# Score broadcasts on GpSimd's queue, row copies for one batch only, later scatters and earlier transposes in an attention and mixture-of-depths kernel

## The chip, the cores and the metric

The kernel runs on one core of one Trainium2 chip. The metric is the device time of one execution in microseconds. Three timed runs of the kernel before gave 152.77, 153.0 and 153.94 us, median 153.0. The profiled execution has a span of 148.8 us; all positions in time below are microseconds from the start of that span.

TensorE (PE) multiplies matrices, VectorE (DVE) and ScalarE (ACT) do elementwise work, GpSimd (POOL) does casts, small copies and the issue of its own transfers, and SyncE (SP) only issues transfers.

## What is computed

There are four batches of 768 rows. Attention with 8 heads of size 64 looks at a window of 128 rows and at the first 4 rows ("sinks"). Its output `x` is stored, and then, for each batch, the 128 rows with the highest gate score go through a small two-layer network and are added to.

```
scores = q @ k.T / sqrt(64)              # kept where key < 4, or 0 <= query - key < 128
a      = softmax(scores);  x = a @ v     # x: [4, 768, 512], heads side by side
s      = x @ w_gate                      # [4, 768]
out    = x
for b in range(4):
    top = the 128 rows with the largest s[b]
    xe  = x[b, top]
    ye  = relu(xe @ w1) @ w2             # 512 -> 1024 -> 512
    out[b, top] = xe + sigmoid(s[b, top])[:, None] * ye
```

## The kernel before

The work is a list of 30 units. Units 0 to 11 are batch 0 (two halves of the heads, six blocks of 128 rows each); units 12 to 17 are batch 1, 18 to 23 batch 2, and 24 to 29 batch 3, one block of 128 rows with all heads each. Everything else is hung onto these units in four places: `before` (first), `middle` (after the score matmuls), `at` (after the unit's values and its norm) and `late` (last). Each engine executes its instructions in the order in which the program emits them.

```python
for i, (b, j, g) in enumerate(steps):
    for f in early.get(i, []): f()          # before(i, ...)
    if i: store(i - 1)                      # rows of unit i-1 to out (and a copy)
    step_scores(i + 2)                      # PE: q.k for the unit after next; ACT: exp into pt
    for f in mid.get(i, []): f()            # middle(i, ...)
    values(b, j, heads, X, g or 0)          # PE: sinks (vsk, psk), then pt @ v, into two banks X
    ...
    norm(x, heads, X)                       # DVE: reciprocal and multiply, X -> x
    for f in todo.get(i, []): f()           # at(i, ...)
    ...    gate_score(b, j, x)              # DVE: one column of scol (when g != 0)
    for f in todo_late.get(i, []): f()      # late(i, ...)
```

The q and k of a batch arrive as float32 (`raw`), are cast by GpSimd to bfloat16 (`kq`, three pairs of buffers), transposed by PE into the banks Y, and copied to SBUF (`KT`, `QT`) by DVE and ACT. A batch's first scores are emitted two units ahead of its first unit.

```python
def transposes(b, hp, bank):     # PE: 6 + 6 transposes; then the copies KT (DVE or ACT) and QT (ACT)
for b, i0 in ((1, 6), (2, 12), (3, 18)):
    for hp in range(HP):
        before(i0 + hp - 2, lambda b=b, hp=hp: cast_pair(b, hp))        # POOL
        at(i0 + hp, lambda b=b, hp=hp: transposes(b, hp, Y))
        at(i0 + hp, lambda b=b, hp=hp: sink_keys(b, hp))                # POOL
    at(i0 + 4, lambda b=b: sink_scores(b, range(HP), 0, Y))
```

To rank a score within its batch, every partition needs all 768 scores. For batches 0 and 1 the scores go out to DRAM and come back broadcast to 128 partitions:

```python
def bounce_out(b): sp.dma_start(out=srow[b, :]..., in_=st[b].scol[:, :])
def bounce_in(b):  sp.dma_start(out=sbc[:, :], in_=srow[b, :].partition_broadcast(128))
def rank_c(b, c):  dve.tensor_scalar(..., in0=sbc[:, :], scalar1=st[b].scol[:, c:c + 1], ..., op0=ALU.is_gt, ...)

for b, i, js in ((0, 12, (15, 15, 16, 17, 17, 18)), (1, 18, (20, 21, 22, 23, 24, 25))):
    middle(i, lambda b=b: bounce_out(b))
    middle(i + 1, lambda b=b: bounce_in(b))
    for c, i_c in enumerate(js):
        late(i_c, lambda b=b, c=c: rank_c(b, c))
```

For batches 2 and 3 PE spreads each column (`spread`, into bank 2) and DVE compares it (`compare`). After the ranks come `choose` (PE and DVE: the row numbers of the chosen rows; GpSimd: `gather`), `ffn_cast`, `ffn_in`, `ffn_1`, `ffn_2` and `ffn_out`. The rows of batches 1 to 3 are stored twice, to `out` and to `xrow[b]`, and gathered from the copy:

```python
def store(i):
    sp.dma_start(out=out[b, j * 128:(j + 1) * 128, :], in_=xt[(b, j)])
    if b: sp.dma_start(out=xrow[b][j * 128:(j + 1) * 128, :], in_=xt[(b, j)])
def ffn_out(b, bank):
    dve.scalar_tensor_tensor(out=y[:, :], in0=ps[:, bank, :], scalar=gt[b][:, 0:1], in1=xe[b % 3][:, :], ...)
    pool.indirect_dma_start(out=flat[0:(b + 1) * S, :], out_offset=... idx[b] ..., in_=y[:, :], ...)   # scatter
```

[...]

Of the kernel before, what the change touches and what calls it, by code (L numbers as in the profile page):

```python
# [8 lines left out]
FP32 = mybir.dt.float32  # L9
BF16 = mybir.dt.bfloat16  # L10
I32 = mybir.dt.int32
U32 = mybir.dt.uint32
# [3 lines left out]
B = 4  # L16
H = 8
S = 768
D = 64
HP = H // 2  # L20
NB = S // 128
DM = H * D
# [11 lines left out]
def kernel(  # L34
# [14 lines left out]
    pe, dve, act, pool, sp = nc.tensor, nc.vector, nc.scalar, nc.gpsimd, nc.sync  # L49
# [4 lines left out]
    jp = ctx.enter_context(tc.tile_pool(name="jp", bufs=2))  # L54
# [6 lines left out]
    X, Y = 4, 6  # L61
# [10 lines left out]
    x0 = one([128, NB, DM], FP32, "x0")  # L72
    scolb = [one([128, NB], FP32, f"scol{i}") for i in range(B)]
    xb = x0[:, 0:NB // 2, :].bitcast(BF16).rearrange("p a (t n) -> p (a t) n", t=2)
    E2 = x0[:, NB - 1, :].bitcast(BF16)[:, 0:NB * 128].rearrange("p (c n) -> p c n", n=128)
    sbc = one([128, S], FP32, "sbc")
# [8 lines left out]
    tok = [one([128, NB, 4], BF16, f"tok{i}") for i in range(B)]  # L85
    gt = [one([128, 1], FP32, f"gt{i}") for i in range(B)]
    idx = [one([128, 1], U32, f"idx{i}") for i in range(B)]
# [18 lines left out]
    tk_i = one([128, B + 1, NB], I32, "tk_i")  # L106
    flat = out.rearrange("b s d -> (b s) d")
    srow = tc.dram_tile([B, S], FP32, name="srow")
    xrow = [None] + [tc.dram_tile([S, DM], FP32, name=f"xrow{i}") for i in range(1, B)]
    idl = [None] + [x0[:, NB - 2, 8 * i:8 * i + 1].bitcast(U32) for i in range(1, B)]  # L110

    class State:
        def __init__(self, b):
# [52 lines left out]
    def transposes(b, hp, bank):  # L166
        s = st[b]
        n = slot[(b, hp)]
        for t, (src, dst) in enumerate(((kq[2 * n], s.KT), (kq[2 * n + 1], s.QT))):
            trp = ps[:, bank + t, :].bitcast(BF16).rearrange("p (c n) -> p c n", c=8)  # L170
            for c in range(NB):
                pe.transpose(out=trp[:, c, :], in_=src[:, c, :, :].rearrange("p h d -> p (h d)"),  # L172
                             identity=ident_b[:, :])
            o = dst[:, hp, :].rearrange("d (p c) -> d p c", c=NB)
            i = trp[:, 0:NB, :].rearrange("d c p -> d p c")
            if t == 0 and (b == 0 or hp % 2 == 0):
                dve.tensor_copy(out=o, in_=i)  # L177
            else:
                act.copy(out=o, in_=i)  # L179
# [123 lines left out]
                                 op0=ALU.mult, op1=ALU.add, accum_out=st[b].scol[:, j:j + 1])  # L303

    def bounce_out(b):
        sp.dma_start(out=srow[b, :].rearrange("(p c) -> p c", c=NB), in_=st[b].scol[:, :])

    def bounce_in(b):
        sp.dma_start(out=sbc[:, :], in_=srow[b, :].partition_broadcast(128))

    def rank_c(b, c):
        dve.tensor_scalar(out=junk[:, :].bitcast(BF16)[:, 0:S], in0=sbc[:, :], scalar1=st[b].scol[:, c:c + 1],  # L312
# [35 lines left out]
    def chosen(b, bank, e=E):  # L348
        t = tok[b]
        for c in range(NB):  # L350
            pe.matmul(out=ps[:, bank, 0:4], lhsT=e[:, c, :], rhs=t[:, c, :],
                      start=(c == 0), stop=(c == NB - 1))
        ch = jp.tile([128, 4], FP32, name="ch", tag="ch")
        dve.tensor_copy(out=ch[:, :], in_=ps[:, bank, 0:4])
        dve.tensor_scalar(out=(idl[b] if b else idx[0])[:, :], in0=ch[:, 0:1], scalar1=128.0, scalar2=ch[:, 1:2],
                          op0=ALU.mult, op1=ALU.add)
        if b:
            chl = x0[:, NB - 2, 32:33]
            dve.tensor_scalar_add(out=chl[:, :], in0=ch[:, 1:2], scalar1=float(b * S))
            dve.tensor_scalar(out=idx[b][:, :], in0=ch[:, 0:1], scalar1=128.0, scalar2=chl[:, 0:1],  # L360
                              op0=ALU.mult, op1=ALU.add)
        return ch
# [6 lines left out]
    def gate_end(b):  # L369
        g = gt[b]  # L370
        dve.tensor_scalar_add(out=g[:, :], in0=g[:, :], scalar1=1.0)
        dve.reciprocal(out=g[:, :], in_=g[:, :])

    def gather(b):
        src, ix = (xrow[b], idl[b]) if b else (flat, idx[0])
        pool.indirect_dma_start(out=xe[b % 3][:, :], out_offset=None, in_=src[0:S, :],
                                in_offset=bass.IndirectOffsetOnAxis(ap=ix[:, 0:1], axis=0),
                                bounds_check=S - 1, oob_is_err=False)

    def ffn_cast(b):  # L380
        pool.tensor_copy(out=xeb[:, :], in_=xe[b % 3][:, :])
# [16 lines left out]
    def ffn_2(b, half, bank):  # L398
        for f in range(4):
            fc = 4 * half + f  # L400
            pe.matmul(out=ps[:, bank, :], lhsT=hT[:, fc, :], rhs=w2_sb[:, fc, :],
                      start=(fc == 0), stop=(fc == 7))

    def ffn_out(b, bank):
        y = jp.tile([128, DM], FP32, name="y", tag="y")
        dve.scalar_tensor_tensor(out=y[:, :], in0=ps[:, bank, :], scalar=gt[b][:, 0:1], in1=xe[b % 3][:, :],  # L406
                                 op0=ALU.mult, op1=ALU.add)
        pool.indirect_dma_start(out=flat[0:(b + 1) * S, :],
                                out_offset=bass.IndirectOffsetOnAxis(ap=idx[b][:, 0:1], axis=0),
                                in_=y[:, :], in_offset=None, bounds_check=(b + 1) * S - 1, oob_is_err=False)  # L410

    with tc.manual_schedule():
        dve.memset(zb[:, :], 0.0)
# [59 lines left out]
        def at(i, f):  # L473
            todo.setdefault(i, []).append(f)
# [7 lines left out]
        def before(i, f):  # L482
            early.setdefault(i, []).append(f)
# [13 lines left out]
        xt = {}  # L497

        def store(i):
            b, j, g = steps[i]  # L500
            if g == 0:
                return
            sp.dma_start(out=out[b, j * 128:(j + 1) * 128, :], in_=xt[(b, j)])
            if b:
                sp.dma_start(out=xrow[b][j * 128:(j + 1) * 128, :], in_=xt[(b, j)])


        arrived = {}
# [19 lines left out]
        def choose(b, bank, e=E):  # L528
            keep[b] = chosen(b, bank, e)
            gate(b, keep[b])  # L530
            gather(b)
# [23 lines left out]
        at(26, lambda: choose(1, 3))  # L555
        late(26, lambda: select(E2, rankl[0], 0, NB))
        at(27, lambda: gate_end(1))
        at(27, lambda: choose(2, 2, E2))
        at(28, lambda: gate_end(2))
        for b in range(B - 1):  # L560
            at((12, 18, 24)[b], lambda b=b: token_cols(b))
# [7 lines left out]
        for b, at_ in ((1, (0, 1, 2, 3)), (2, (6, 8, 9, 11)), (3, (13, 14, 15, 16))):  # L569
            for hp, i in enumerate(at_):  # L570
                before(i, lambda b=b, hp=hp: load_pair(b, hp))
        at(2, lambda: transposes(0, 1, Y))
        at(3, lambda: transposes(0, 3, Y))
        at(3, lambda: sink_keys(0, 1))
        at(3, lambda: sink_keys(0, 3))
        at(4, lambda: sink_scores(0, (1, 3), 1, Y))
        for b, i0 in ((1, 6), (2, 12), (3, 18)):
            for hp in range(HP):
                before(i0 + hp - 2, lambda b=b, hp=hp: cast_pair(b, hp))
                at(i0 + hp, lambda b=b, hp=hp: transposes(b, hp, Y))  # L580
                at(i0 + hp, lambda b=b, hp=hp: sink_keys(b, hp))
            at(i0 + 4, lambda b=b: sink_scores(b, range(HP), 0, Y))

        def ffn(b, i):
            before(i, lambda: ffn_cast(b))
            at(i, lambda: ffn_in(b, Y))
            at(i + 1, lambda: ffn_1(b, 0, Y + 1))
            at(i + 1, lambda: ffn_1(b, 1, Y))
            for half in range(2):
                at(i + 2, lambda half=half: ffn_2(b, half, Y + 1))  # L590
            at(i + 2, lambda: ffn_out(b, Y + 1))
        ffn(0, 24)
        ffn(1, 27)
        before(29, lambda: ffn_cast(2))
        at(29, lambda: ffn_in(2, Y))

# [15 lines left out]
        for i, (b, j, g) in enumerate(steps):  # L612
            for f in early.get(i, []):
                f()
            if i:
                store(i - 1)
            step_scores(i + 2)
            for f in mid.get(i, []):
                f()
            heads = range(4) if g is None else (2 * g, 2 * g + 1)  # L620
            values(b, j, heads, X, g or 0)
            if b == 0:
                x = x0[:, j, :]
            else:
                x = xp.tile([128, DM], FP32, name="x", tag="x")[:, :]
            norm(x, heads, X)
            if i == len(steps) - 1:
                gate_score(b, j, x)
            for f in todo.get(i, []):
                f()  # L630
            if g != 0:
                xt[(b, j)] = x
                if i < len(steps) - 1:
                    gate_score(b, j, x)
                if b == B - 1:
                    pool.tensor_copy(out=xb[:, j, :], in_=x)  # L636
            for f in todo_late.get(i, []):
                f()
            if i == 5:
                pool.iota(iota_i[:, :], pattern=[[1, 128]], base=0, channel_multiplier=0)  # L640
                pool.iota(tk_i[:, 0:B, :], pattern=[[0, B], [1, NB]], base=0, channel_multiplier=0)
                pool.iota(tk_i[:, B, :], pattern=[[0, NB]], base=0, channel_multiplier=1)
            if i == 8:
                dve.tensor_copy(out=iota_f[:, :], in_=iota_i[:, :])
                for n in range(B):
                    dve.tensor_copy(out=tok[n][:, :, 0], in_=tk_i[:, n, :])
                    dve.tensor_copy(out=tok[n][:, :, 1], in_=tk_i[:, B, :])
        store(len(steps) - 1)

# [19 lines left out]
        choose(b, 2)  # L669
        ffn_2(2, 1, 0)  # L670
        ffn_out(2, 0)
        gate_end(b)
        ffn_1(b, 0, Y)
        ffn_1(b, 1, Y + 1)
        ffn_2(b, 0, 1)
        ffn_2(b, 1, 1)
        ffn_out(b, 1)


# [33 lines left out]
```

The softmax here doesn't subtract the row's maximum and nothing guards it: scores larger than these inputs give would overflow.

## Time and profile before

| engine | busy us of 148.8 | share |
|---|---|---|
| PE (matmul) | 120.2 | 81% |
| DVE | 91.5 | 62% |
| ACT | 78.5 | 53% |
| POOL | 58.8 | 40% |

The core moved 35.57 MB: 30.16 MB on SyncE's queue, and 4.23 MB on GpSimd's. The 18 stores to `xrow` are 256 KB each, as are the 24 to `out`. A share of busy time is an average over the whole span; where time can be won is read from the order of events around each wait. The useful views are the table of waits (who waited for whom), the timeline of one engine (start, duration, engine, line, operation, count of merged instructions, and in brackets the idle time ahead of it and what ended it), and the page's rows of 40 slices, in which each slice stands for 3.7 us.

### The profile page before, as it was taken

The numbers are of one execution on the slowest core, as the hardware profiler recorded it, in microseconds if no ns is written. First come the engines' busy times: TensorE is split into PE (matmuls) and PEld (weight loads), VectorE is DVE, ScalarE is ACT, GpSimd is POOL, SyncE is SP. The second block draws the span as 40 slices with busy tenths as digits, with TensorE's granted clock in tenths as the row PEclk, the third lists the DMA queues.
The fourth block names the chain that finished last, engine by engine and source line by source line (L and its number), as shares of the span: only waits on it lengthen the run. The fifth ranks groups of instructions, "written<-read, shape, count | busy, mean of one in ns | idle before, by whom it ended". The sixth has DMA issues, their size and how long they took to land. (4 is left out here: it accounts for less than half of the span.)

```text
span 148.8 us, 6421 instructions
## 1 busy us (share of the span) xinstructions
PE 120.2 (81%) x2755; PEld 91.6 (62%) x2759; DVE 91.5 (62%) x287; ACT 78.5 (53%) x106; POOL 58.8 (40%) x99
## 2 busy tenths in 40 slices
PE   6687989998989987669799920998989969977940
PEld 2255676787778866538588810776777558856810
DVE  6851172569438464098988306778996696688520
ACT  3169467598887875365746780055827232323310
POOL 8819404865504573343170401810111264412421
PEclk9999999999999999999999997589999999999995
DMA  3999969987999999999999799899995346332031
GB/s 100 376 222 361 213 173 365 341 207 194 286 291 375 335 240 317 352 347 348 268 327 316 221 257 317 218 194 172 279 275 195 143 148 216 141 141 77 3 138 70
DMA packets 43227, 35.57 MB, mean 239 GB/s; under 512 B 27184, under 2 KB 36400, under 8 KB 43200
## 3 DMA queue, kind: packets, MB, share of 16 engines
q1 hardware_dynamic: 40288, 30.16, 66.8%
q0 software_dynamic: 2368, 4.23, 13.6%
q10 hardware_dynamic: 544, 0.79, 1.5%
q8 instruction: 21, 0.34, 0.9%
q14 instruction: 6, 0.05, 0.1%
HBM read 25.20 MB, written 12.06 MB: 250 GB/s over the span
## 5 line engine op out<-in xcount | busy, mean ns | idle before, releaser
L251 ACT ACTIVATE pt<-ps 128x1024 f32<-128x1024 f32 x48 | 47.0, 1032 | 6.7 <-PE ps L229 6.0
L262 PE MATMUL ps<-vbuf,pt 64*64 64x65 f32 (+1 forms) x1440 | 47.6, 230 | 3.6 <-issue 2.9
L262 PEld LDWEIGHTS ps<-vbuf,pt 64*64 64x64 f32 (+1 forms) x1440 | 40.7, 139 | 15.3 <-issue 11.8
L141 POOL CAST kq<-raw 128x768 bf16<-128x768 f32 x28 | 23.4, 847 | 20.4 <-DMA raw<-in_k_dram 14.9
L295 DVE RECIPROCAL rz<-ps 128x8 f32<-128x8 f32 (+1 forms) x30 | 5.9, 196 | 29.1 <-PE ps L262 29.0
L272 PE MATMUL ps<-vsk,psk 64*64 64x260 f32 (+1 forms) x180 | 16.5, 359 | 8.6 <-DVE x L298 8.6
L213 PE MATMUL ps<-QT,KT 64*64 64x192 bf16 (+2 forms) x384 | 17.2, 243 | 5.0 <-ACT QT L179 2.6
L298 DVE TENSOR_TENSOR x<-ps,rz 128x256 f32<-128x256 f32 (+1 forms) x60 | 19.5, 366 | 1.6 <-DMA xrow<-x 0.4
L312 DVE TENSOR_SCALAR_CACHE_REDUCE junk<-sbc,scol 128x768 bf16<-128x768 f32 x12 | 12.2, 1013 | 12.3 <-DMA sbc<-srow 11.9
L302 DVE CUSTOM_DVE_ANT_0 junk<-x,wgb 128x512 f32<-128x512 f32 x24 | 18.0, 750 | 0.4
L186 POOL COPY ksk<-KT 64x4 bf16<-64x4 bf16 x32 | 8.7, 273 | 23.8 <-DVE KT L177 12.5
L179 ACT COPY QT<-ps 128x768 bf16<-128x768 bf16 x16 | 12.8, 801 | 7.9 <-PE ps L172 7.9
L213 PEld LDWEIGHTS <-KT 64*64 64x64 bf16 x384 | 10.3, 105 | 9.9 <-issue 6.0
L229 PE MATMUL ps<-mask,ident_b 64*64 64x256 bf16 (+1 forms) x208 | 15.0, 259 | 0.0
L172 PE MATMUL ps<-ident_b,kq 128*128 128x128 bf16 x192 | 13.6, 220 | 1.6 <-ACT kq L139 1.5
L272 PEld LDWEIGHTS ps<-vsk,psk 64*64 64x64 f32 x180 | 7.7, 135 | 10.3 <-DVE x L298 8.9
L172 PEld LDWEIGHTS <-kq 128*128 128x128 bf16 x192 | 11.1, 98 | 3.7 <-ACT kq L139 1.7
L318 ACT COPY sbl<-ps 128x128 f32<-128x128 f32 x12 | 3.1, 261 | 19.3 <-PE ps L316 19.3
L177 DVE COPY KT<-ps 128x768 bf16<-128x768 bf16 x10 | 9.5, 950 | 1.4 <-PE ps L172 1.4
L636 POOL CAST x<-x 128x512 bf16<-128x512 f32 x6 | 4.2, 703 | 15.1 <-DVE x L298 9.0
L394 PE MATMUL ps<-xeT,w_sb 128*128 128x128 bf16 x128 | 8.0, 219 | 0.7 <-ACT xeT L387 0.7
L394 PEld LDWEIGHTS <-w_sb 128*128 128x128 bf16 x128 | 7.4, 98 | 1.1 <-DVE y L406 0.9
(91 smaller groups left out, 133.1 us busy)
## 6 DMA issues: line engine op xcount, KB each, us to landing
out_dram<-x SPq DMA_DIRECT2D x24, 256.0 KB, 4.7
raw<-in_k_dram SPq DMA_DIRECT2D x15, 384.0 KB, 5.5
raw<-in_q_dram SPq DMA_DIRECT2D x15, 384.0 KB, 5.9
xrow<-x SPq DMA_DIRECT2D x18, 256.0 KB, 4.9
vbuf<-in_v_dram SPq DMA_DIRECT2D x33, 128.0 KB, 5.2
w_sb<-in_moe_w_dram POOLq DMA_DIRECT2D x4, 512.0 KB, 12.5
vbuf<-in_v_dram SPq DMA_DIRECT2D x2, 384.0 KB, 6.8
sbc<-srow SPq DMA_DIRECT2D x2, 384.0 KB, 6.6
```

Source lines behind the costliest of these rows:

```text
L141: (eng or pool).tensor_copy(out=o, in_=i)
L172: pe.transpose(out=trp[:, c, :], in_=src[:, c, :, :].rearrange("p h d -> p (h d)"), identity=ident_b[:, :])
L179: act.copy(out=o, in_=i)
L213: pe.matmul(out=sc[64 * m:64 * m + 64, e, a, o:o + n], lhsT=s.KT[r, hp, k0:k0 + 64], rhs=s.QT[r, hp, k0:k0 + n], start=a == 0, stop=False, ...
L229: pe.matmul(out=o, lhsT=ident_b[r, r], rhs=w[r].unsqueeze(1).to_broadcast((64, a.stop - a.start, 2, 64)), start=False, stop=True, skip_gro ...
L251: act.activation(out=po[:, gi, :, :, :], in_=sc[:, :, :, :], func=ACT.Exp, scale=0.125)
L262: pe.matmul(out=ps[64 * c:64 * c + 64, bank + be, hh * SK:hh * SK + SK], lhsT=p[i][rows, h, 64 * slot:64 * slot + 64], rhs=s.v[be][rows, h ...
L272: pe.matmul(out=ps[64 * c:64 * c + 64, bank + be, a * SK:z * SK], lhsT=s.psk[which][r, c, 64 * (j - 1):64 * j], rhs=vsk[r, b, be, a:z, :], ...
L298: dve.tensor_tensor(out=xo[:, e, :, :], in0=xg[:, e, :, 0:D], in1=rz[:, e, 0:n, :].to_broadcast((128, n, D)), op=ALU.mult)
L302: dve.tensor_tensor_reduce(out=junk[:, :], in0=x, in1=wgb[:, :], scale=1.0, scalar=0.0, op0=ALU.mult, op1=ALU.add, accum_out=st[b].scol[:, ...
L312: dve.tensor_scalar(out=junk[:, :].bitcast(BF16)[:, 0:S], in0=sbc[:, :], scalar1=st[b].scol[:, c:c + 1], scalar2=0.0, op0=ALU.is_gt, op1=A ...
L394: pe.matmul(out=hps[:, f, :], lhsT=w1_sb[:, dc, fc * 128:(fc + 1) * 128], rhs=xeT[:, dc, :], start=(dc == 0), stop=(dc == 3), skip_group_c ...
```

## The change

Five things are changed.

1. The two transfers of a score broadcast, out and back, are issued by GpSimd instead of SyncE, at the same places of the program. They are to leave the crowded queue of loads and stores.
2. Only the last batch is copied to `xrow`: 12 of the 18 copies, 256 KB each, go. Batches 1 and 2 are gathered from `out` itself, so `tok` now holds row numbers that count from the start of `out`, and the separate local row number is made only for the last batch.
3. The scatter is taken out of `ffn_out`. Those of batches 0 and 1 come at the end of units 28 and 29, behind the gathers of batches 1 and 2, which now read the tensor that the scatters write.
4. The transposes of a unit go from after its values and norm (`at`) to before its sinks and values (`middle`), so that the copies of KT and QT lie beside the value matmuls.
5. `choose(2)` uses bank 3 instead of bank 2, in which `spread` works.

```diff
-    xrow = [None] + [tc.dram_tile([S, DM], FP32, name=f"xrow{i}") for i in range(1, B)]
+    xrow = tc.dram_tile([S, DM], FP32, name="xrow")
 ...
     def bounce_out(b):
-        sp.dma_start(out=srow[b, :].rearrange("(p c) -> p c", c=NB), in_=st[b].scol[:, :])
+        pool.dma_start(out=srow[b, :].rearrange("(p c) -> p c", c=NB), in_=st[b].scol[:, :])
     def bounce_in(b):
-        sp.dma_start(out=sbc[:, :], in_=srow[b, :].partition_broadcast(128))
+        pool.dma_start(out=sbc[:, :], in_=srow[b, :].partition_broadcast(128))
 ...
     def chosen(b, bank, e=E):
-        dve.tensor_scalar(out=(idl[b] if b else idx[0])[:, :], in0=ch[:, 0:1], ...)
-        if b:
+        last = b == B - 1
+        dve.tensor_scalar(out=(idl if last else idx[b])[:, :], in0=ch[:, 0:1], ...)
+        if last:
             (two more DVE instructions)
 ...
     def gather(b):
-        src, ix = (xrow[b], idl[b]) if b else (flat, idx[0])
+        src, ix, n = (xrow, idl, S) if b == B - 1 else (flat, idx[b], (b + 1) * S)
 ...
     def ffn_out(b, bank):
         dve.scalar_tensor_tensor(out=y[:, :], ...)
+    def scatter(b):
         pool.indirect_dma_start(out=flat[0:(b + 1) * S, :], ...)
 ...
-            if b:
-                sp.dma_start(out=xrow[b][j * 128:(j + 1) * 128, :], in_=xt[(b, j)])
+            if b == B - 1:
+                sp.dma_start(out=xrow[j * 128:(j + 1) * 128, :], in_=xt[(b, j)])
 ...
-        at(27, lambda: choose(2, 2, E2))
+        at(27, lambda: choose(2, 3, E2))
 ...
-        at(2, lambda: transposes(0, 1, Y))
-        at(3, lambda: transposes(0, 3, Y))
+        middle(2, lambda: transposes(0, 1, Y))
+        middle(3, lambda: transposes(0, 3, Y))
 ...
-                at(i0 + hp, lambda b=b, hp=hp: transposes(b, hp, Y))
+                middle(i0 + hp, lambda b=b, hp=hp: transposes(b, hp, Y))
 ...
+        late(28, lambda: scatter(0))
+        late(29, lambda: scatter(1))
 ...  (after the last unit: scatter(2) and scatter(3) follow their ffn_out)
```

More of the change, by code (lines that the diff above doesn't have):

```diff
@@ L108 @@
     srow = tc.dram_tile([B, S], FP32, name="srow")
-    xrow = [None] + [tc.dram_tile([S, DM], FP32, name=f"xrow{i}") for i in range(1, B)]
-    idl = [None] + [x0[:, NB - 2, 8 * i:8 * i + 1].bitcast(U32) for i in range(1, B)]
+    xrow = tc.dram_tile([S, DM], FP32, name="xrow")
+    idl = x0[:, NB - 2, 0:1].bitcast(U32)
     class State:
@@ L354, in chosen @@
         dve.tensor_copy(out=ch[:, :], in_=ps[:, bank, 0:4])
-        dve.tensor_scalar(out=(idl[b] if b else idx[0])[:, :], in0=ch[:, 0:1], scalar1=128.0, scalar2=ch[:, 1:2],
+        last = b == B - 1
+        dve.tensor_scalar(out=(idl if last else idx[b])[:, :], in0=ch[:, 0:1], scalar1=128.0, scalar2=ch[:, 1:2],
                           op0=ALU.mult, op1=ALU.add)
-        if b:
+        if last:
             chl = x0[:, NB - 2, 32:33]
@@ L374, in gather @@
     def gather(b):
-        src, ix = (xrow[b], idl[b]) if b else (flat, idx[0])
-        pool.indirect_dma_start(out=xe[b % 3][:, :], out_offset=None, in_=src[0:S, :],
+        src, ix, n = (xrow, idl, S) if b == B - 1 else (flat, idx[b], (b + 1) * S)
+        pool.indirect_dma_start(out=xe[b % 3][:, :], out_offset=None, in_=src[0:n, :],
                                 in_offset=bass.IndirectOffsetOnAxis(ap=ix[:, 0:1], axis=0),
-                                bounds_check=S - 1, oob_is_err=False)
+                                bounds_check=n - 1, oob_is_err=False)
     def ffn_cast(b):
@@ L402, in ffn_2 @@
                       start=(fc == 0), stop=(fc == 7))
+    ys = {}
     def ffn_out(b, bank):
-        y = jp.tile([128, DM], FP32, name="y", tag="y")
+        y = ys[b] = jp.tile([128, DM], FP32, name="y", tag="y")
         dve.scalar_tensor_tensor(out=y[:, :], in0=ps[:, bank, :], scalar=gt[b][:, 0:1], in1=xe[b % 3][:, :],
                                  op0=ALU.mult, op1=ALU.add)
+    def scatter(b):
         pool.indirect_dma_start(out=flat[0:(b + 1) * S, :],
                                 out_offset=bass.IndirectOffsetOnAxis(ap=idx[b][:, 0:1], axis=0),
-                                in_=y[:, :], in_offset=None, bounds_check=(b + 1) * S - 1, oob_is_err=False)
+                                in_=ys[b][:, :], in_offset=None, bounds_check=(b + 1) * S - 1, oob_is_err=False)
     with tc.manual_schedule():
@@ L640 @@
                 pool.iota(iota_i[:, :], pattern=[[1, 128]], base=0, channel_multiplier=0)
-                pool.iota(tk_i[:, 0:B, :], pattern=[[0, B], [1, NB]], base=0, channel_multiplier=0)
+                pool.iota(tk_i[:, 0:B, :], pattern=[[NB, B], [1, NB]], base=0, channel_multiplier=0)
                 pool.iota(tk_i[:, B, :], pattern=[[0, NB]], base=0, channel_multiplier=1)
@@ L645 @@
                 for n in range(B):
-                    dve.tensor_copy(out=tok[n][:, :, 0], in_=tk_i[:, n, :])
+                    dve.tensor_copy(out=tok[n][:, :, 0], in_=tk_i[:, n % (B - 1), :])
                     dve.tensor_copy(out=tok[n][:, :, 1], in_=tk_i[:, B, :])
@@ L671 @@
         ffn_out(2, 0)
+        scatter(2)
         gate_end(b)
@@ L677 @@
         ffn_out(b, 1)
+        scatter(b)
 _INS = ['q', 'k', 'v', 'n_sink', 'window', 'moe_w_gate', 'moe_w1', 'moe_w2', 'moe_capacity']
```

## The prediction

> **What bounds the kernel now.** I read the table of waits first, then the timelines of PE, DVE, SyncE and GpSimd around each long wait, then the rows of slices. PE is busy 81% and almost never idle between 10 and 130 us, so its idle stretches are the time to be won. The table of waits:
>
> ```profile
> DVE junk L312 <- DMA sbc<-srow: 11.9, 2, 7.6
> POOL ksk L186 <- DMA xe<-out_dram,idx: 5.9, 1, 5.9
> PE ps L272 <- DVE x L298: 8.6, 5, 5.5
> PE ps L213 <- ACT QT L179: 2.6, 4, 0.8
> PE ps L316 <- DVE ch L354: 1.2, 1, 1.2
> PE ps L213 <- DVE KT L177: 0.7, 1, 0.7
> ```
>
> Columns: microseconds in total, times, longest. DVE waits only twice for the broadcast scores, but for 11.9 us, and PE's 8.6 us behind DVE's `x` is the echo. PE around the worst of them:
>
> ```profile
> 87.08 0.27 PE L213 MATMUL ps<-QT,KT 64*64 64x192 bf16 x2 [0.81 <-ACT QT L179]
> ...
> 92.93 1.46 PE L272 MATMUL ps<-vsk,psk 64*64 64x260 f32 x8 [5.47 <-DVE x L298]
> 94.32 3.08 PE L262 MATMUL ps<-vbuf,pt 128*64 128x65 f32 x64
> ...
> 99.11 0.61 PE L272 MATMUL ps<-vsk,psk 64*64 64x260 f32 x8
> 99.65 1.78 PE L262 MATMUL ps<-vbuf,pt 128*64 128x65 f32 x64
> ```
>
> The idle 5.47 us are followed by value matmuls that take 4.47 us (92.93 to 97.40) where the same group takes 2.32 (99.11 to 101.43). The row of granted clocks has its only deep dip there:
>
> ```profile
> PEclk9999999999999999999999997589999999999995
> ```
>
> DVE shows the cause, SyncE where the broadcast came from:
>
> ```profile
> 63.00 1.01 DVE L312 TENSOR_SCALAR_CACHE_REDUCE junk<-sbc,scol 128x768 bf16<-128x768 f32 x1 [4.27 <-DMA sbc<-srow]
> 70.46 0.08 DVE L302 DVE_READ_ACCUMULATOR2_ANT scol<- 128x1 f32 x1
> 90.70 1.01 DVE L312 TENSOR_SCALAR_CACHE_REDUCE junk<-sbc,scol 128x768 bf16<-128x768 f32 x1 [7.63 <-DMA sbc<-srow]
> ```
>
> ```profile
> 51.38 0.38 SPq L306 DMA_DIRECT2D srow<-scol  x1
> 56.18 0.32 SPq L309 DMA_DIRECT2D sbc<-srow  x1
> 80.22 0.41 SPq L306 DMA_DIRECT2D srow<-scol  x1
> 83.97 0.32 SPq L309 DMA_DIRECT2D sbc<-srow  x1
> ```
>
> Batch 1's last score is ready at 70.5, but its transfer is issued only at 80.22: SyncE's queue is in order and that far behind. The broadcast then takes 83.97 to 90.7. In that stretch the transfers themselves are the limit (DMA row at 9 in nearly every slice up to 100 us), and `raw` sets when GpSimd can cast:
>
> ```profile
> 45.18 1.80 POOL L141 CAST kq<-raw 128x768 bf16<-128x768 f32 x2 [4.80 <-DMA raw<-in_k_dram]
> 48.87 0.83 POOL L141 CAST kq<-raw 128x768 bf16<-128x768 f32 x1 [1.89 <-DMA raw<-in_k_dram]
> ```
>
> [...] 5.47 us idle, then a granted clock of 0.50 over 92.93 to 97.40. [...] The trace has one GpSimd transfer in the crowded stretch, the gather of batch 0: 7.7 us from issue to landing, against 3.6 for the later gathers, so being in the other queue does not make a transfer quick. [...] The gather at 82.42 took 1.63 us to issue against about 1.05 for the others; I allow a microsecond for it, though nothing here shows the cause.
>
> **The change part by part.**
>
> *Broadcast of batch 1.* GpSimd's program has it behind the cast of pair (3,2), which ends at 71.2, just after the score (70.5). Issue at 71.3 plus about 0.7 (GpSimd's direct issues take 0.66 to 0.79) and some 4 us to land is 76. The way back stands behind the cast of (3,3), which now ends at 77.3 and should end at 75 to 77; with 0.8 to issue and 5 to 7 to land, the scores are there at 81 to 84. DVE wants them at 83.1, perhaps 81.5 with the other gains. PE had 7.63 − 5.47 = 2.16 us of slack against that wait, so little of it is left: I keep 0.7 us. Gain: 5.47 + (4.47 − 2.32) − 0.7 = 6.9 us.
>
> *Broadcast of batch 0.* GpSimd reaches the outward transfer behind the cast of (2,2), at 50.9; SyncE did at 51.4. The way back is behind the cast of (2,3), 54.1, and behind the landing, about 55. So it comes only 1 to 2 us earlier, 61 against 63. PE's idle behind `x` after it are 1.34 + 0.27 + 0.86 = 2.5 us; of these I expect 1.5 to go.
>
> *Copies.* 12 × 256 KB = 3.1 MB of 35.6 MB, at the mean 239 GB/s 13 us of transfer time, half of it before 85 us. Nothing on PE waits for a store directly (DVE 0.4 us once), so it counts only as making the previous two possible, and for `raw`. No separate gain.
>
> *Transposes.* Four waits of a batch's first scores for fresh KT or QT go: 0.71 at 22.6, 0.77 at 37.5, 0.81 at 59.0 and 0.81 at 87.1, 3.1 us. But the transposes move forward by the length of a unit's values (1.4 us in batch 0, 2.4 later), and the casts don't. The cast of (1,2) ends at 31.7 and PE would be there at 30.9; that of (2,1) ends at 47.0 and PE would be there at about 45, where the transposes before stood at 48.2. They now hold up the value matmuls behind them. I give back 1.5 of the 3.1 us. Gain 1.6.
>
> *Bank 3.* At 122.40 PE waits 1.22 us for DVE's copy out of bank 2; gone, while the next operand (the cast that ends at 121.8) allows about 1.0.
>
> *Scatters and index arithmetic.* Four DVE instructions of 0.14 to 0.21 us go, off the path; the scatters of batches 0 and 1 were not waited for. At the end the same two scatters follow the same chain of ranks, network and last sum (143.35). Nothing.
>
> *Given back later.* Everything behind 93 us comes earlier, but the weights do not quite: before, they were issued at 93.6 to 95.8 (behind the sink keys, which wait 5.9 us for the gather, and a load of v) and the last landed 18.1 us after its issue, at 113.9, for a use at 116.1: 2 us of slack. With some 9 us gained they must come as much earlier; the gather is issued only 1 to 2 us earlier, but lands sooner. I charge 0.7.
>
> Sum: 6.9 + 1.5 + 1.6 + 1.0 − 0.7 = 10.3 us. 153.0 − 10.3 = 142.7; as the losses are less certain to be complete than the gains, I say 143.2.
>
> **The rivals.** First, the wait only moves: GpSimd now stops on the outward transfer and on crowded DMA, its broadcast lands at 88 or later, and sink keys, gather and weights behind it are late as well. For it: 7.7 us for the gather, 12.5 for the weights. Against it: the 9.7 us in which the batch 1 scores lay ready on SyncE's side are gone in any case. It would leave 147 to 149 us. Second, DMA is the bound up to 100 us, and PE, no longer held by DVE, is held by casts: for it the DMA row and 14.9 us of GpSimd's wait for `raw`; against it the casts of batch 3, which have 8 to 10 us of slack (65.7 + 0.8 = 66.5 for transposes at 76.2). It costs at batch 2 only, and more than my 1.5 us would mean 145 to 146. Third, the weights become the wait: if they still come at 106 and 114, PE stands still from 102 and most of the gain is given back, 149. Against it: their trigger, the last gather and v loads, comes earlier with fewer copies in the way.
>
> **Range and chances.** All parts at their best give about 140.5, the first two rivals in mild form 147. Every rival still leaves part of the 6.9 us, so a slower kernel would need a new stall of more than 10 us. Range 140.5 to 147.0; faster by over 2% 0.93, within 0.05, slower 0.02.
>
> **What would show each step.** In the new profile, DVE's wait for `sbc` should fall from 11.9 to under 4 us, with the wait at batch 1 under 2.5; the dip of the granted clock near 93 us should be gone; PE's waits for QT and KT at a batch's first scores should fall to nearly nothing; new waits of the transposes (L172) for GpSimd or for its casts should appear near 31 and 46 us, 1 to 2 us in all; the wait of L316, the spread, for `ch` should be gone. The step on the weights is wrong if PE waits over 1.5 us ahead of `ffn_1` or `ffn_2` of batch 0. The whole is wrong if `sbc` of batch 1 still lands after 88 us[...].

## The result and the profile after

The changed kernel took 145.81 us (median of 4 runs, 144.11 to 147.16) against 152.88 for the kernel before beside it; the ratio is 0.946, with a 95% interval of 0.934 to 0.957. Its profiled execution has a span of 142.4 us, against 148.8. Medians below are over all runs of a kernel; ratios and their intervals leave out runs that were disturbed and longer, and the profiles of the transposes alone, of all but the transposes, of the copies alone and of the repeated kernel after are of such runs.

The table of waits of the kernel after (microseconds in total, times, longest), with the old waits and the new ones:

```profile
PE ps L262 <- issue: 4.6, 5, 1.5
...
POOL ksk L186 <- DMA xe<-out_dram,idx: 3.4, 1, 3.4
...
DVE junk L312 <- DMA sbc<-srow: 2.4, 2, 2.2
...
PE ps L172 <- DVE KT L177: 1.5, 2, 1.3
...
PE ps L272 <- DVE x L298: 1.4, 4, 0.5
...
PE ps L213 <- ACT sbl L318: 0.9, 1, 0.9
...
PE ps L213 <- ACT QT L179: 0.2, 1, 0.2
```

DVE's wait for the broadcast fell from 11.9 to 2.4 us, PE's echo behind `x` from 8.6 to 1.4, and the waits for QT and KT ahead of first scores nearly went. The wait of `spread` for `ch` is gone. Three lines are new or grown: PE waits for DVE's copy of KT (1.5), for ACT's copy into `sbl` (0.9), and 4.6 us with no releaser ("issue": nothing that the profile shows was missing), where the kernel before has 2.9.

The timeline of PE at the old stall (start, duration, engine, line, operation, count), and the row of granted clocks:

```profile
88.32 0.69 PE L272 MATMUL ps<-vsk,psk 64*64 64x260 f32 x7
88.94 1.92 PE L262 MATMUL ps<-vbuf,pt 128*64 128x65 f32 x64
...
92.44 0.61 PE L272 MATMUL ps<-vsk,psk 64*64 64x260 f32 x8
92.98 1.78 PE L262 MATMUL ps<-vbuf,pt 128*64 128x65 f32 x64
```

```profile
PEclk9999999999999999999999999999999999999995
```

Nothing stands idle ahead of 88.32, and the 64 value matmuls behind it take 1.92 us instead of 3.08: the stall and the dip that followed it are both gone. The broadcast itself, from the timelines of GpSimd and DVE:

```profile
70.97 0.55 POOL L306 DMA_DIRECT2D srow<-scol  x1 [2.52 <-DVE scol L302]
77.79 0.54 POOL L309 DMA_DIRECT2D sbc<-srow  x1 [1.98 <-DVE rz L295]
```

```profile
83.61 1.01 DVE L312 TENSOR_SCALAR_CACHE_REDUCE junk<-sbc,scol 128x768 bf16<-128x768 f32 x1 [0.25 <-DMA sbc<-srow]
```

Where the time came from is read from the starts of units (the first matmul of a unit's sinks, L272), before against after:

| stretch | before, us | after, us | won, us |
|---|---|---|---|
| start to unit 21 | 82.26 | 84.39 | −1.3 |
| unit 21 to 23 | 16.85 | 8.05 | +8.0 |
| unit 23 to 27 | 19.36 | 19.03 | +0.3 |
| unit 27 to 28 | 4.57 | 3.59 | +1.0 |
| unit 28 to the end | 25.76 | 27.34 | −1.6 |
| span | 148.8 | 142.4 | +6.4 |

In the first two rows 0.84 us is corrected for: after, unit 21's own transposes stand ahead of its start, before they stood behind it. The 8 us are where the prediction put them. But 84 us of program, with two stalls less, ended later than before. The new waits there, from the timeline of PE (the bracket is the idle time ahead of the instruction, and what ended it):

```profile
62.05 0.69 PE L262 MATMUL ps<-vbuf,pt 64*64 64x65 f32 x30 [1.40 <-issue]
...
68.52 0.28 PE L262 MATMUL ps<-vbuf,pt 64*64 64x65 f32 x3 [1.54 <-issue]
...
73.71 0.83 PE L172 MATMUL ps<-ident_b,kq 128*128 128x128 bf16 x12 [1.29 <-DVE KT L177]
...
83.19 0.33 PE L213 MATMUL ps<-QT,KT 64*64 64x128 bf16 x8 [0.90 <-ACT sbl L318]
```

The third is a bank of the transposes: DVE's copy of KT of unit 18 (72.71) stands behind two comparisons of batch 0 (70.71 and 71.77), and PE's next transposes start only at 73.71, when it is done. The fourth is bank 2: ACT's copy (82.89) stands behind the gate's exponential (82.78), which waits for DVE. The table of stretches shows what the transfers do there (stretch, its length, busy time and count of each engine, granted clock, share of the 16 DMA engines, GB/s); first the kernel before, then the one after:

```profile
60.00:85.00 25.00, 21.14 (x571) 16.91 (x568) 18.32 (x48) 14.39 (x19) 9.18 (x13) 1.00 1.03 309
85.00:100.00 15.00, 8.72 (x168) 6.51 (x166) 7.41 (x23) 5.22 (x8) 4.17 (x8) 0.77 0.97 250
```

```profile
60.00:85.00 25.00, 19.64 (x502) 15.10 (x498) 20.01 (x52) 13.56 (x18) 8.43 (x14) 1.00 0.91 265
85.00:100.00 15.00, 13.82 (x372) 11.00 (x370) 12.02 (x40) 9.57 (x15) 4.93 (x9) 1.00 0.95 203
```

Between 60 and 85 us DMA has less to do (309 to 265 GB/s), and PE still does less work (21.14 to 19.64 us). Between 85 and 100 it does 5.1 us more.

### The profile page after: what moved, and what is told of

It is laid out like the page before. It is cut to its first block, busy times and chain, and to the rows that moved or that the text cites. A ratio compares the mean times of both kernels' runs of the same rounds, so it can differ in the third digit from the quotient of the medians.

```text
span 142.4 us, 6406 instructions
## 1 busy us (share of the span) xinstructions
PE 120.0 (84%) x2759; PEld 89.9 (63%) x2759; DVE 92.0 (65%) x283; ACT 78.7 (55%) x106; POOL 60.5 (43%) x103
## 5 line engine op out<-in xcount | busy, mean ns | idle before, releaser
L262 PE MATMUL ps<-vbuf,pt 64*64 64x65 f32 (+1 forms) x1440 | 46.9, 227 | 4.6 <-issue 4.6
L262 PEld LDWEIGHTS ps<-vbuf,pt 64*64 64x64 f32 (+1 forms) x1440 | 39.9, 135 | 15.8 <-issue 13.3
L272 PE MATMUL ps<-vsk,psk 64*64 64x260 f32 (+1 forms) x180 | 16.3, 356 | 1.5 <-DVE x L298 1.4
L229 PE MATMUL ps<-mask,ident_b 64*64 64x256 bf16 (+1 forms) x208 | 15.6, 259 | 0.3 <-issue 0.3
L213 PEld LDWEIGHTS <-KT 64*64 64x64 bf16 x384 | 10.9, 106 | 6.5 <-issue 5.2
L186 POOL COPY ksk<-KT 64x4 bf16<-64x4 bf16 x32 | 7.9, 248 | 15.1 <-DVE KT L177 9.3
L643 POOL CAST x<-x 128x512 bf16<-128x512 f32 x6 | 4.7, 791 | 13.7 <-DVE x L298 8.5
L272 PEld LDWEIGHTS ps<-vsk,psk 64*64 64x64 f32 x180 | 6.9, 131 | 4.3 <-DVE x L298 1.7
L229 PEld LDWEIGHTS <-ident_b 64*64 64x64 bf16 x208 | 8.8, 106 | 0.6 <-issue 0.6
L323 DVE TENSOR_SCALAR_CACHE_REDUCE G<-sbl,scol 128x128 bf16<-128x128 f32 (+5 forms) x12 | 8.1, 674 | 0.9 <-ACT sbl L318 0.9
```

What stands on the lines that cost most here:

```text
L213: pe.matmul(out=sc[64 * m:64 * m + 64, e, a, o:o + n], lhsT=s.KT[r, hp, k0:k0 + 64], rhs=s.QT[r, hp, k0:k0 + n], start=a == 0, stop=False, ...
L229: pe.matmul(out=o, lhsT=ident_b[r, r], rhs=w[r].unsqueeze(1).to_broadcast((64, a.stop - a.start, 2, 64)), start=False, stop=True, skip_gro ...
L262: pe.matmul(out=ps[64 * c:64 * c + 64, bank + be, hh * SK:hh * SK + SK], lhsT=p[i][rows, h, 64 * slot:64 * slot + 64], rhs=s.v[be][rows, h ...
L272: pe.matmul(out=ps[64 * c:64 * c + 64, bank + be, a * SK:z * SK], lhsT=s.psk[which][r, c, 64 * (j - 1):64 * j], rhs=vsk[r, b, be, a:z, :], ...
```

## The experiments

The experiments form three sets. Each set has its own runs of the kernel before on the same chip, and only kernels of one set are compared closely; the medians of the kernel before were 153.08, 151.37 and 152.51 us in the three sets. "Before" and "after" in the diffs say which kernel was edited.

### First set: one part alone, or all but one

**The broadcasts alone.** Before, with

```diff
-        sp.dma_start(out=srow[b, :]..., in_=st[b].scol[:, :])
+        pool.dma_start(out=srow[b, :]..., in_=st[b].scol[:, :])
-        sp.dma_start(out=sbc[:, :], in_=srow[b, :].partition_broadcast(128))
+        pool.dma_start(out=sbc[:, :], in_=srow[b, :].partition_broadcast(128))
```

> The kernel before with one part of the change: the score broadcasts of batches 0 and 1 are issued by GpSimd. All 18 row copies, the transposes and the banks are as before. Theory A (the broadcast of batch 1 is nearly the whole gain, whatever else is in the queues): the 5.5 us stall of PE ahead of unit 22 and the slow clock after it go, 145.5 to 147.5 us. Rival C (the broadcast came sooner only because 12 copies had gone): it still lands after 86 us, PE still waits 3 us or more for DVE there, 149 to 152 us.

It took 152.1 us, ratio 0.996 (0.991 to 1.002): hardly anything, though the wait that it was aimed at went. Neither theory had this: the wait went as A said, and the time stayed about where C had it. DVE waits 0.7 us for `sbc`, and PE no more than 0.5 us behind `x`. PE's longest waits are now these, and the row of clocks has two dips:

```profile
71.14 0.28 PE L262 MATMUL ps<-vbuf,pt 64*64 64x65 f32 x3 [2.03 <-issue]
...
116.23 1.86 PE L401 MATMUL ps<-w_sb,hT 128*128 128x512 bf16 x4 [2.40 <-DMA w_sb<-in_moe_w_dram]
```

```profile
PEclk9999999999999999999559999999999699999995
```

In place of the 5.47 us this profile has more waits with no releaser (6.7 us in all, against 3.6 in the kernel before), 6.8 us at half clock behind the longest of them, and a wait for the weights with a dip of its own.

**The transposes alone.** Before, with the moves of part 4 of the change (`at` to `middle` for all transposes).

> The kernel before with one part of the change: the transposes moved in front of a unit's sinks and values. Theory A (they earn nothing, because PE then waits for the bank that DVE's late KT copy holds[...]): 152 to 154 us, with the QT waits of 0.8 us gone and a new wait of a transpose for a KT copy of over 1 us around 74 us. Rival B (each part earns its predicted share): 151.0 to 151.8 us.

It took 153.8 us, ratio 1.003 (0.995 to 1.011). The waits for QT are gone, and in their place the profile has the wait of transposes for DVE's KT (1.0) and that of scores for ACT's `sbl` (0.9). Neither is in the kernel before, so the moved transposes bring both with them.

**All but the transposes.** After, with part 4 taken back.

> The changed kernel with the transposes back where they were, all else changed. Theory A: 144.5 to 146 us, no slower than the changed kernel or even faster, with the 0.8 us QT waits back and the 1.3 us wait of a transpose for a KT copy gone. Rival B: 147 to 148 us, 1.6 us slower than the changed kernel.

It took 143.82 us, ratio 0.938 (0.931 to 0.945). QT waits of 2.6 us are back; the waits for KT's bank and for `sbl` are gone. Its interval overlaps that of the kernel after, so as far as these runs show, one set of waits is as dear as the other.

**All but GpSimd's broadcasts.** After, with

```diff
-        pool.dma_start(out=srow[b, :]..., in_=st[b].scol[:, :])
+        sp.dma_start(out=srow[b, :]..., in_=st[b].scol[:, :])
-        pool.dma_start(out=sbc[:, :], in_=srow[b, :].partition_broadcast(128))
+        sp.dma_start(out=sbc[:, :], in_=srow[b, :].partition_broadcast(128))
```

> The changed kernel with the score broadcasts back on SyncE's queue; copies, scatters, transposes and bank as changed. Theory A: the stall at batch 1 is back, some us shorter as the queue has 6 copies fewer ahead of it: PE waits 2 to 5 us ahead of unit 22, 149 to 152 us. Rival C (the missing copies alone pull the broadcast in): PE waits under 1 us there, 145 to 147 us.

It took 146.02 us, ratio 0.941 (0.932 to 0.951), so the broadcast on SyncE costs nothing once the copies are out. SyncE's timeline, and two lines of the table of waits:

```profile
76.46 0.38 SPq L306 DMA_DIRECT2D srow<-scol  x1
79.46 0.34 SPq L309 DMA_DIRECT2D sbc<-srow  x1
```

```profile
DVE junk L312 <- DMA sbc<-srow: 4.2, 2, 2.9
...
PE ps L272 <- DVE x L298: 1.8, 5, 0.5
```

The way back is issued 4.5 us sooner than before (79.46 against 83.97), and what DVE still waits no longer reaches PE: 0.5 us at most.

### Second set: the copies

**The copies alone.** Before, with parts 2 and 3 of the change and nothing else.

> The kernel before with the copies of batches 1 and 2 gone (and the gathers from the output and the later scatters that this needs); broadcasts on SyncE, transposes, and bank 2 as before. Theory D, new after the first four runs (the row copies are the gain: [...]with them in the queue any one wait that goes is paid elsewhere): 144.5 to 147 us, PE waits under 1.5 us for DVE ahead of unit 22. Rival E (it takes two parts together, copies gone and either the broadcast moved or the transposes moved): 148.5 us or more.

It took 145.15 us against 151.37, ratio 0.968 (0.955 to 0.982). By the medians this one part earns most of the gain, as theory D said. Its profile (146.8 us of span) misses the other half of that forecast: DVE still waits 5.49 us for the scores of batch 1 and PE 3.42, not under 1.5, so the part doesn't always remove that stall. What the shorter executions look like isn't known.

**Issues or bytes.** After, with the 12 missing copies put back as spare copies that nobody reads, once whole (256 KB each), once 8 numbers of each row, and once whole for batch 2 alone:

```diff
+            if 0 < b < B - 1:          # third kernel: if b == 2
+                sp.dma_start(out=spare[b - 1][j * 128:(j + 1) * 128, :], in_=xt[(b, j)][:, :])
+                # second kernel: columns 0:8 on both sides
```

> The changed kernel with 12 copies of rows (batches 1 and 2, 256 KB each, to a spare buffer that nobody reads) put back on SyncE's queue; everything else as changed. Theory D: 150.5 to 153 us, so nearly all of the gain goes though no wait of any computation was put back. Rival E and the prediction's own view (copies earn nothing by themselves): 145 to 147 us.

> As the run before, but each of the 12 extra transfers moves 8 floats per row (4 KB instead of 256 KB): the issues and their places in the queue are back, the bytes are not. If the bytes cost, 145 to 147 us like the changed kernel. If the in-order queue costs (12 more issues and slots), 149 us or more.

> The changed kernel with the 6 full extra copies of batch 2 alone, stored from unit 19 on. Theory D with the crowded stretch up to about 90 us as the place: a small part comes back, 146 to 148 us, mostly through the weights (PE waits 1 to 3 us for them around ffn_1 or ffn_2 of batch 0). If the copies of batch 2 are as costly as those of batch 1: 148.5 to 150 us.

| spare copies | MB | us, median (range) | ratio |
|---|---|---|---|
| 12, of 8 numbers a row | 0.05 | 143.77 (142.42 to 146.0) | 0.961 (0.945 to 0.976) |
| 6, whole | 1.6 | 146.25 (143.67 to 147.64) | 0.978 (0.963 to 0.993) |
| 12, whole | 3.1 | 148.03 (145.78 to 152.21) | too few for an interval |

The issues cost nothing that can be seen. The bytes cost some 4.3 us by the medians; the size is rough, with five runs each, but the ranges with tiny and with whole copies overlap by only 0.2 us. With 6 copies the range overlaps both others widely, so how the loss divides between the batches isn't shown. Theory D is right in kind and wrong in size: it had 150.5 to 153 us with all the bytes back, and 148.03 came, by the medians still 3.3 us less than the kernel before, though the ranges overlap. So the bytes account for somewhat more than half of the 7.6 us that the kernel with tiny copies gains in this set. The rest would be the work of the other parts, though queue and transposes earned nothing alone; which of them or which combination (bank 3 and the scatters were never tried by themselves) isn't shown.

In the profile with all 12 whole copies DVE waits 2.6 us for a spare copy to leave `x`, and PE, by way of `sbl`, stands still:

```profile
84.69 0.47 PE L214 MATMUL ps<-QT,KT 64*64 64x128 bf16 x8 [2.93 <-ACT sbl L319]
```

The granted clock is 0.5 from 83.9 to 90.8 us. With 6 copies PE waits 0.93 us for the weights instead (theory D had 1 to 3). The bytes are paid for in different waits in the two.

### Third set: the new waits taken away

**Two instructions put earlier.** After, with one comparison of batch 0 a unit earlier (so that KT's copy stands behind one less) and `spread` ahead of a unit's other work (so that ACT's copy precedes the gate's exponential):

```diff
-        for b, i, js in ((0, 12, (15, 15, 16, 17, 17, 18)), ...):
+        for b, i, js in ((0, 12, (15, 15, 16, 16, 17, 18)), ...):
-                at(start(b) + j + 1, lambda j=j: spread(b, j, 2))
+                todo.setdefault(start(b) + j + 1, []).insert(0, lambda j=j: spread(b, j, 2))
```

> The kernel after, with two things put earlier in a queue: DVE compares column 3 of batch 0 in unit 16 instead of 17, so that the copy of KT of unit 18 stands behind one comparison less, and the spread of a unit goes ahead of the unit's other work, so that ACT's copy into sbl no longer stands behind the gate's exponential. Theory D (the moved transposes and the broadcast gained little because new waits of PE for DVE and ACT took the gain): the waits L172 <- DVE KT (1.29 us at 73.7) and L213 <- ACT sbl (0.90 us at 83.2) fall under 0.4 us each, and the time falls by 1.5 to 2.2 us against the kernel after of this call, to about 144. Rival E (what is saved before 100 us is taken back behind it, by the weights[...]): both waits go, yet the time falls by under 0.7 us, and PE waits over 0.8 us for w_sb ahead of a network unit, or its waits with no releaser grow by over 1 us.

It took 147.37 us, ratio 0.947 (0.937 to 0.957). After once more, in the same set, took 144.27 with 0.949. Both waits went as planned: KT's is 0.3 us at most, and `sbl`'s is off the list. Nothing was earned that the runs could show. The timeline of PE in this kernel:

```profile
63.74 0.75 PE L262 MATMUL ps<-vbuf,pt 64*64 64x65 f32 x30 [2.22 <-issue]
...
108.16 1.30 PE L262 MATMUL ps<-vbuf,pt 128*64 128x65 f32 x46 [1.19 <-issue]
```

A table of stretches has the dip behind the first of them; the granted clock is the third number from the end. The first profile of the kernel after has 1.00 at the same place, but the repeated one (the second line) has 0.50 as well, so the edit isn't what brought the dip:

```profile
65.00:67.00 2.00, 2.00 (x34) 1.42 (x34) 1.93 (x5) 1.21 (x2) 0.83 (x1) 0.50 1.02 351
```

```profile
65.00:67.00 2.00, 2.00 (x30) 1.22 (x28) 1.66 (x5) 0.58 (x1) 0.43 (x1) 0.50 0.95 325
```

**The same without the moved transposes, and with SyncE's broadcasts.** Two edits of the kernel above.

> The run above with the transposes put back behind a unit's values. Theory D: with the wait for KT's copy gone, the moved transposes do earn what the waits for fresh QT are worth, so this one is 0.8 to 2 us slower than the run above, with 2 to 3 us of PE's waits for QT. Rival E: within 0.7 us of it, although the waits for QT are back.

> The first run of this call with the broadcasts back on SyncE's queue. Theory D (the missing copies alone pull SyncE's broadcast of batch 1 in): within 1 us of the first, either way; DVE's wait for sbc 4 to 5 us, PE's wait behind x at batch 1 under 1 us. The prediction's own step (the queue is what earns): 3 us or more slower, with PE waiting over 3 us behind x near 87 us.

They took 145.66 us, ratio 0.959 (0.952 to 0.966), and 145.68, ratio 0.960 (0.953 to 0.967). The first has its QT waits of 2.4 us back, as expected; by the medians it is 1.7 us faster than with the transposes moved, by the ratios 1.2% slower: nothing is decided. In the second DVE waits only 0.7 us for `sbc`, less than I expected; the step of the prediction that it was to test asked for 3 us or more, and the medians and ratios show between −1.7 us and +1.3%.

**After once more.**

The forecast is about PE's waits with no releaser.

> The kernel after once more, to have it beside the others on one chip. All theories: 144 to 147 us. [...]the two longest of them are again in unit 16 at 62 us and near 68.5 us, at the same counts of value matmuls (30 left of a group of 64, and 3 left); if they hang on chance, they are elsewhere.

It took 144.27 us. Its three longest waits without a releaser, from the timeline of PE:

```profile
64.03 1.14 PE L262 MATMUL ps<-vbuf,pt 64*64 64x65 f32 x30 [1.95 <-issue]
...
70.78 0.28 PE L262 MATMUL ps<-vbuf,pt 64*64 64x65 f32 x3 [1.13 <-issue]
...
104.92 0.68 PE L262 MATMUL ps<-vbuf,pt 64*64 64x65 f32 x28 [1.53 <-issue]
```

The first two are 2 us later than in the first profile but at the same instructions: 30 left of a group of 64, and 3 left. The forecast of the two longest was half right: the second longest is now the one at 104.92, which the first profile has too, with 0.72 us and the same 28 left.

No kernel of the study is faster than the one after by more than its runs vary. With the copies out and their bytes not put back, eight kernels have medians of 143.8 to 147.4 us, with ratios of 0.938 to 0.968.

## Why the prediction was right, and where it was not

The time was right: 143.2 was said, 145.81 and, in a later set, 144.27 came, inside the range. The marks that it set for itself were met, except the new waits for casts. The reasons were partly wrong, and the marks couldn't show it. That the number fell inside is therefore in part luck: between the two profiles, the 8.0 us at batch 1 are as foreseen, but −1.3 us stand up to unit 21, where some 2.3 were expected, and −1.6 behind unit 28, where nothing was. The lower end of the range, 140.5, isn't the sum of its parts at their full sizes either: 7.6 + 2.5 + 3.1 + 1.0 would give 138.8.

*Copies: the step that failed.* The prediction let them count only as making room for the broadcasts and for `raw`, with "no separate gain", as nothing on PE waits for a store. Alone they make 3.2% (0.968; 1.8 to 4.5%), where the finished kernel with tiny spare copies makes 4.0% in the same set, and putting their bytes back into the finished kernel takes away some 4.3 us. That no engine waits for a store says only that stores are not the last to arrive. Their bytes take time of the same 16 DMA engines: between 85 and 100 us their busy share is 1.00 at 257 GB/s with 12 whole spare copies, and 0.94 at 208 GB/s with tiny ones.

*Broadcasts, 6.9 + 1.5.* The size at batch 1 was right (8.0 us between units 21 and 23, with the 0.8 of its QT wait, against 7.7 foreseen), and so was the landing at 83.6. What was wrong is its cause. With the queue changed alone, 0.4% came of it; with all but the queue changed, 5.9%. The queue alone removes the stall; the missing bytes do so beside the other parts (all but GpSimd's broadcasts), while 3.42 us of it are left in the profile of the copies alone. Only the missing bytes bring time by themselves. The prediction credited the issuing engine; that was its author's estimate. With that engine alone changed, DVE's wait for `sbc` went from 11.9 to 0.7 us, and the time stayed at 152.1 us, ratio 0.996. At batch 0 PE's waits behind `x` fell from 2.5 to 0.5 us: more than the 1.5 foreseen, but not kept.

*Transposes, +1.6.* The 3.1 us of waits for KT and QT went. What was to be given back, 1.5 us of waits for casts near 31 and 46 us, is not there: the only one is 0.34 us at 27.40 us. In its place come 1.29 us for KT's bank and 0.90 for bank 2. I had looked at the engine that feeds the transposes and not at the queues that empty their banks. That these two belong to the moved transposes is shown by the kernels that have them with the move alone and lose them without it.

*Up to unit 21* the prediction had 1.5 for batch 0, and 0.8 of the 1.6; measured, −1.3. Gone are 2.0 us behind `x` and 2.3 for QT and KT. New are 1.29 + 0.90 + 0.34, and waits with no releaser grew from 1.95 to 4.03: 4.3 us gone against 4.6 new. The last microsecond lies in gaps too small for the tables.

*Bank 3, +1.0.* The stretch in which it lies is 1.0 shorter; alone it was not tried. *Scatters and index arithmetic, 0:* not tried apart from the copies. *Weights, −0.7:* nothing in the kernel after waits for them. They do become the wait in two kernels with more bytes (2.40 and 0.93 us), as the third rival had it. *The end:* 1.6 us were lost behind unit 28 that no step had. Of these, DVE's wait for `sbl` at 127.65 (0.86, new) and PE's for `hT` at 135.86 (0.48, new) could be about half; the rest was not pursued.

*The rivals.* The first fell: the broadcast is there before 84 us. The second, DMA as the bound, gave the best time (145 to 146), and the spare copies support its core. But PE is not held by the casts, as it said; it is held by different things in turn, among them waits with no releaser (4.6 us at L262 in the kernel after; see the last section).

*What the third set adds.* With 2.2 us of PE's waits taken away, the time did not fall. Where they went isn't shown. The profile has a longer wait with no releaser than the first one of the kernel after (2.22 us against 1.40) and 3.4 us at half clock behind it, but the repeated kernel after, without the edit, has nearly the same (1.95 us and a dip). What is shown three times (queue alone, transposes, order) is that waits were removed and no time was gained. That it is the full DMA that takes the time back is only supported by the spare copies (some 4.3 us for 12 whole ones): a kernel with far fewer bytes was not tried.

## What to carry to other kernels

When the DMA row is full, count the bytes that can go before moving waits about: here 12 stores of 256 KB that no one waited for cost some 4.3 us. A wait that is removed can come back under another name (here 2.3 us for QT and KT went, and 1.29 + 0.90 came), so a part's worth is measured by doing it alone and by leaving it alone out, not by the length of the wait it removes. And if an operation is moved ahead, look at who has to empty its output as well as at who feeds it.

## What the runs showed of the hardware

**PE's waits with no releaser, counted in PE's instructions.** The group with 30 matmuls left in unit 16 waits 1.21 us in the kernel before, 1.40 and 1.95 in the two profiles of after, and from nothing to 2.36 in edits; one with 28 left in unit 25 waits 0.72 us in the kernel before and in the first profile of after, and 1.53 in the second. The traces of before and after have 12 such waits of 0.15 us or more, of 0.20 to 1.54 us. In the trace of before they come when 2241, 2497, 4033, 4289 and 4545 of PE's instructions, weight loads included, have started; in that of after, when 705, 961, 2497, 2753, 3521, 4033 and 4289 have. All these counts are multiples of 256 apart. The queues of the trace include one named "instruction", in both with 21 packets, 0.34 MB in all. Its packets (count, MB, share of 16 engines) in the half microsecond from 59.5 us in the kernel after, then in that from 61.0 us in the kernel with two instructions put earlier:

```profile
q8 instruction: 1, 0.02, 11.1%
```

```profile
q8 instruction: 1, 0.02, 11.0%
```

PE stops at 60.65 us in the one and goes on at 62.05; in the other it stops at 61.52 and goes on at 63.74. The next packet in the kernel after lies between 66.0 and 66.5; PE stops at 66.98 and goes on at 68.52. In the traces of before and after, all 12 waits end 2.18 to 2.47 us after such a packet starts. Waits and packets lie together in time; that the ones cause the others isn't shown, as no kernel of the study moved the packets themselves. In the crowded stretch the waits reach 2.36 us (the kernel with tiny spare copies, at 64.00), while behind 115 us the traces of before and after have none of 0.15 or more.

**A clock of 0.50 followed 1.75 us without a matmul in one stretch of 3.42 us, and a clock of 1.00 followed 1.71 us in another.** In the trace of the kernel before the clock changes at 90.81, 97.63 and 145.42 us: 6.83 and 47.79 us apart, which is 2 and 14 times 3.41. The first lines are the stretch ahead of its dip, with 3.34 us without a matmul, and the two of the dip itself; then come the one with the next longest time without a matmul, 1.61 us, and what followed it (after the length stands PE's busy time; the clock is the third number from the end):

```profile
87.39:90.80 3.41, 0.08 (x4) 0.00 (x0) 0.10 (x1) 1.49 (x2) 0.50 (x3) 1.00 1.04 289
90.80:94.21 3.41, 1.28 (x8) 0.58 (x8) 3.27 (x13) 0.00 (x0) 0.69 (x2) 0.50 0.83 271
94.21:97.63 3.42, 3.42 (x67) 3.07 (x66) 1.76 (x6) 0.00 (x0) 2.98 (x5) 0.50 0.96 219
```

```profile
5.47:8.88 3.41, 1.80 (x17) 1.08 (x17) 2.67 (x8) 1.99 (x3) 1.74 (x6) 1.00 1.20 324
8.88:12.30 3.42, 2.84 (x47) 1.74 (x45) 1.05 (x2) 2.03 (x4) 1.45 (x3) 1.00 1.12 247
```

Cut into stretches of 3.41 us from where the clock changes, the traces of before and after have 76 at full clock up to some 8 us before their ends. The one with 3.34 us without a matmul was followed by a clock of 0.50; the 75 with 1.61 us or less were not. The two cases nearest to each other, each stretch with the one behind it, are in the third set's kernel with SyncE's broadcasts and in the kernel with 12 whole spare copies:

```profile
69.32:72.74 3.42, 1.67 (x63) 1.34 (x60) 1.63 (x6) 0.71 (x2) 1.33 (x2) 1.00 1.02 270
72.74:76.15 3.41, 3.41 (x42) 3.09 (x42) 3.04 (x7) 2.39 (x3) 0.18 (x1) 0.50 1.06 295
```

```profile
5.44:8.85 3.41, 1.70 (x16) 0.98 (x16) 2.69 (x8) 1.87 (x3) 1.77 (x6) 1.00 1.18 331
8.85:12.27 3.42, 2.96 (x47) 1.83 (x46) 1.05 (x2) 2.03 (x3) 1.33 (x3) 1.00 1.10 236
```

The length of a single wait didn't decide it. One of 2.03 us in the kernel with the broadcasts alone ended at 71.14 us, and 6.8 us at a clock of 0.50 followed; one of the same length in the third set's kernel without the moved transposes ended at 71.16, and the clock stayed at 1.00 from 64 to 77 us.
